# Two x tiles first on one queue: reordering the first loads and the first TensorE work of a gated attention/FFN kernel

## The chip, the cores and the metric

The kernel runs on one core of one Trainium2 chip. The metric is the device time of one execution in microseconds. A time is a median over runs, and two kernels are compared by runs on the same chip in the same rounds. The engines are TensorE (matrix products), VectorE and ScalarE (elementwise work), GpSimd and SyncE (here it only issues loads). A load (DMA) is put on the queue of the engine that issues it: in the traces of before one queue moved 0.82 MB, which is the five tiles of 160 KB that ScalarE issued. The profile counts 16 DMA engines, and its DMA share is the mean over them. A counter, a semaphore, tells of each load's progress; for a tile it is raised 16 times. A tile has landed with its sixteenth report.

## The reference, cut to what matters

```python
x = A_x                                   # (1, 2048, 640) bf16
g = sigmoid((x * gate_w).sum(-1))         # one gate per row
qkv = x @ wqkv                            # 640 -> q, k, v of 640 columns each
pq, pk = phi(q), phi(k)                   # phi(t) = t+1 if t>0 else exp(t), + 1e-6
a = linear_attention(pq, pk, v) @ wo      # 32 heads of 20
b = (gelu(x @ w_gate) * (x @ w_up)) @ w_down
out = g * a + (1 - g) * b
```

The change touches only the start. The rows of `x` come in 16 tiles of 128 rows. For each tile the kernel projects keys and queries with weights that come in five chunks of 128 rows each: `wk` 0 to 4 for keys, `wq` 0 to 4 for queries. One x tile and one weight chunk are each 160 KB.

## The kernel before: the parts that matter

Tiles 0 and 1 are loaded as they are and transposed on TensorE (`T`). Tiles 2 to 15 come through DMA transposes, and the first of these is issued when `wk` chunk 4 has landed. `KM` is a key projection of tile 0 or 1 over given chunks, `QM` the query projection, and `KQ` the joint projection of a tile from 2 on. `warm` issues matmuls whose results nobody reads; they fill waits.

```python
# loads: two issuing queues, SyncE ("sp", the default) and ScalarE ("act")
P.op("act", ... dma_start(touch[0:16, 0:4], A_wqkv[0:128:8, 640:644]))   # a 128-byte first load
load_x(0)
load_wk(0)
load_x(1, "act")
load_wk(1)
load_wk(3)
P.op("act", ... activation(eg[:, 0:1], zero, ACT.Exp))
load_wk(2, "act")
load_wk(4, "act")
P.op("dve", lambda e: e.memset(gw_sb, 0.0), writes=[r_gw])
dma_in(gw_sb[0:5, :], gate_w..., [r_gw], eng="act")
for k in range(KC):                        # KC = 5
    load_wq(k, ("sp", "act")[k % 2])
for i in range(NXN, NT):                   # tiles 2 to 15
    load_xT(i, after=([r_wk[4]] if i == NXN else ()))
...
# TensorE
warm(5, 512)
warm(1, 128)
T(0, [0], 7)                 # transpose of chunk 0 into PSUM bank 7, then a VectorE copy
T(0, [1, 2, 3, 4], 6)
warm(6, 128)
KM(0, [0])
T(1, [0], 7)
T(1, [1, 2, 3, 4], 6)
warm(3, 128)
KM(1, [0])
for k in (1, 2, 3):
    KM(0, [k])
    KM(1, [k])
gate_col()
for k in (4,):
    KM(0, [k])
    KM(1, [k])
for n in range(4):           # tiles 0 and 1: keys, then queries
    if n == 2:
        for k in range(KC):
            QM(2, [k])
            QM(3, [k])
    phi1(n)                  # ScalarE
    phi2(n)                  # VectorE
for i in range(2, NT):
    KQ(i)
...
```

Of the kernel before, what the change touches and what calls it, by code (L numbers as in the profile page):

```python
# [16 lines left out]
KC = D // 128  # L17
# [144 lines left out]
def bass_gated_mix__linear_attn_block__geglu_ffn__prompt_kernel(  # L162
# [63 lines left out]
    with (  # L226
# [8 lines left out]
        with contextlib.ExitStack() as stack:  # L235
            dma_sems = [stack.enter_context(nc.semaphore("s_in%d" % i)) for i in range(n_dma_in)]

            P = _Plan(["pe", "act", "dve", "pool", "sp"])
# [9 lines left out]
            def new_dma_key():  # L248
                k = "in%d" % dma_next[0]
                dma_next[0] += 1  # L250
                return k

            def v16(o, n):
                return pool[:, o:o + n]
# [13 lines left out]
            wk = wkq[:, :, 0:640]  # L268
            wq = wkq[:, :, 640:1281]
# [30 lines left out]
            gw_sb = v16(O_GW, 128)  # L300
# [4 lines left out]
            r_xn = [P.sb("xn%d" % i, R_XN + i * XW, R_XN + (i + 1) * XW) for i in range(NT)]  # L305
# [3 lines left out]
            r_wk = [P.sb("wk%d" % k, R_WK + k * WW, R_WK + k * WW + 640) for k in range(KC)]  # L309
            r_wq = [P.sb("wq%d" % k, R_WK + k * WW + 640, R_WK + k * WW + 1280) for k in range(KC)]  # L310
# [26 lines left out]
            r_gw = P.res("gw")  # L337

            def dma_in(dst, src, writes, reads=(), eng="sp"):
                P.op(eng, lambda e, dst=dst, src=src: e.dma_start(dst, src),  # L340
                     reads=reads, writes=writes, dma=new_dma_key())
# [3 lines left out]
            def load_x(i, eng="sp"):  # L345
                dma_in(x_aug[:, i, 0:640], A_x[0, i * 128:(i + 1) * 128, :], [r_xn[i]], eng=eng)

            def load_wk(k, eng="sp"):
                dma_in(wk[:, k, :], A_wqkv[k * 128:(k + 1) * 128, 640:1280], [r_wk[k]], eng=eng)

            def load_wq(k, eng="sp"):
                dma_in(wq[:, k, 0:640], A_wqkv[k * 128:(k + 1) * 128, 0:640], [r_wq[k]], eng=eng)


            P.op("act", lambda e: e.dma_start(touch[0:16, 0:4], A_wqkv[0:128:8, 640:644]),
                 writes=[P.res("touch")], dma=new_dma_key())
            load_x(0)
            load_wk(0)
            load_x(1, "act")
            load_wk(1)  # L360
            load_wk(3)

            zero = nc.const_aps.tensor(0.0, (128, 1), F32)
            P.op("act", lambda e: e.activation(eg[:, 0:1], zero, ACT.Exp), writes=[r_eg[0]])
            load_wk(2, "act")
            load_wk(4, "act")
            P.op("dve", lambda e: e.memset(gw_sb, 0.0), writes=[r_gw])
            dma_in(gw_sb[0:5, :], gate_w.rearrange("(k p) -> k p", p=128), [r_gw], eng="act")
            for k in range(KC):
                load_wq(k, ("sp", "act")[k % 2])  # L370

            def load_xT(i, after=()):
                P.op("sp", lambda e: e.dma_start_transpose(xT[:, :, i * 128:(i + 1) * 128],
# [12 lines left out]
            for c in range(NHC):  # L386
# [9 lines left out]
                 reads=[r_ones], writes=[r_ident])  # L396
# [16 lines left out]
            def warm(count, n):  # L413
                def fn(e):
                    last = None
                    for w in range(count):
                        last = e.matmul(ps[:, 4, 0:n], one_l, one_r[:, 0:n], start=True, stop=True)
                    return last
                P.op("pe", fn, writes=[bank[4]])
# [4 lines left out]
            def slot(n):  # L424
                return SLOTS[n % 4]

            def T(i, ks, tb):
                def fn(e):
                    last = None
                    for n, k in enumerate(ks):  # L430
                        last = e.transpose(psb[:, tb, n * 128:(n + 1) * 128],
                                           x_aug[:, i, k * 128:(k + 1) * 128], ident)
                    return last
                P.op("pe", fn, reads=[r_xn[i], r_ident], writes=[bank[tb]])
                P.op("dve", lambda e: e.tensor_copy(
                    xT[:, ks[0]:ks[-1] + 1, i * 128:(i + 1) * 128],
                    psb[:, tb, 0:len(ks) * 128].rearrange("p (k s) -> p k s", k=len(ks))),
                    reads=[bank[tb]], writes=[r_xTa[i] if ks[0] == 0 else r_xT[i]])
# [4 lines left out]
            def KM(n, ks):  # L443
                i = seq[n][1]
                b0, b1 = slot(n)

                def fn(e):
                    last = None
                    for k in ks:
                        lhs = xT[:, k, i * 128:(i + 1) * 128]  # L450
                        e.matmul(ps[:, b0, :], lhs, wk[:, k, 0:512], start=(k == 0), stop=(k == KC - 1))  # L451
                        last = e.matmul(ps[:, b1, 0:128], lhs, wk[:, k, 512:640],
                                        start=(k == 0), stop=(k == KC - 1))
                    return last
                P.op("pe", fn, reads=[r_xTa[i] if i < NXN and ks == [0] else r_xT[i]] + [r_wk[k] for k in ks],
                     writes=[bank[b0], bank[b1]])
# [37 lines left out]
            def gate_col():  # L494

                P.op("pe", lambda e: e.matmul(ps[:, 7, 0:5], gw_sb, ident[:, 0:5], start=True, stop=True),
                     reads=[r_gw, r_ident], writes=[bank[7]])
                P.op("dve", lambda e: e.tensor_copy(wq[:, :, 640:641], ps[:, 7, 0:5].unsqueeze(2)),
                     reads=[bank[7]], writes=[r_gcol])
# [4 lines left out]
            warm(1, 128)  # L504
            T(0, [0], 7)
            T(0, [1, 2, 3, 4], 6)
            warm(6, 128)
            KM(0, [0])
            T(1, [0], 7)
            T(1, [1, 2, 3, 4], 6)  # L510
            warm(3, 128)
            KM(1, [0])
            for k in (1, 2, 3):
                KM(0, [k])
                KM(1, [k])
            gate_col()
            for k in (4,):
                KM(0, [k])
                KM(1, [k])
            for n in range(4):  # L520
# [42 lines left out]
            for i in range(2, NT):  # L563
                KQ(i)
                if i == 4:
                    late_constants()
            P.op("dve", lambda e: e.tensor_scalar(gg, eg, 0.5, 0.5, ALU.mult, ALU.add),
                 reads=r_eg, writes=[r_g])
            P.op("dve", lambda e: e.tensor_scalar(omg, eg, -0.5, 0.5, ALU.mult, ALU.add),
                 reads=r_eg, writes=[r_omg])  # L570
# [7 lines left out]
                 reads=[r_omg], writes=[r_od], dma=new_dma_key())  # L578
# [44 lines left out]
            def ME(g):  # L623
# [6 lines left out]
                for c in cs:  # L630
# [8 lines left out]
                 reads=r_pk[0:2], writes=[r_tmp[0]])  # L639
            for i in range(2, NT):  # L640
                P.op("dve", lambda e, i=i: e.tensor_tensor(zacc, zacc, pk[i], ALU.add),  # L641
                     reads=[r_tmp[0], r_pk[i]], writes=[r_tmp[0]])
# [283 lines left out]
```

## Time and profile before

Three runs of the kernel before gave 274.1, 275.38 and 274.25 us. In the trace of one more run (273.55 us, span 272.2 us) the start looks like this:

| event | us from the span's start |
|---|---|
| full clock on TensorE | 3.77 |
| unbroken stream of key projections begins | 5.18 |
| query projections of tiles 0 and 1 begin | 7.67 |
| joint projections (tile 2) begin | 10.39 |

The page says how the whole span is shared. The first number after an engine is its busy time; the last line shown is the chain of waits by engine.

```profile
span 272.2 us, 3426 instructions
...
PE 267.9 (98%) x1343; PEld 128.1 (47%) x1369; DVE 141.8 (52%) x251; ACT 75.9 (28%) x132; POOL 30.0 (11%) x28
...
PE 95%; DVE 2%; DMA 1%; issue 1%; ACT 1%; SPq 0%; DVEq 0%; ACTq 0%
```

In these lines DVE is VectorE, ACT ScalarE, POOL GpSimd, PE TensorE, PEld its weight loads, and a q stands for an engine's issuing of loads. TensorE bounds the kernel. Only time in which TensorE does nothing useful can be won, and at the start that is the time before the key stream.

Lines of TensorE's timeline of before. The columns are start, duration, engine, source line, operation, output and inputs, shape and count; in brackets is idle time just before and what ended it. L431 are transposes, L417 warm-up matmuls, L451 and L452 key projections, L466 query projections, L536 joint projections.

```profile
3.02 0.74 PE L431 MATMUL ps<-pool 128*128 128x128 bf16 x5
...
4.38 0.38 PE L451 MATMUL ps<-pool 128*128 128x512 bf16 x1 [0.21 <-DMA pool<-in_A_wqkv_dram]
...
4.64 0.44 PE L431 MATMUL ps<-pool 128*128 128x128 bf16 x5
...
5.18 0.39 PE L451 MATMUL ps<-pool 128*128 128x512 bf16 x1
...
7.67 0.38 PE L466 MATMUL ps<-pool 128*128 128x512 bf16 x1
...
10.39 1.89 PE L536 MATMUL ps<-pool 128*128 128x512 bf16 x8
```

Five transposes take 0.74 us at 3.02 and 0.44 us at 4.64. That is the clock: half rate first (0.107 us from one to the next), full rate later (0.055); the trace's record of full clock begins at 3.77.

### The profile page before, as it was taken

The numbers are of one execution on the slowest core, as the hardware profiler recorded it, in microseconds if no ns is written. First come the engines' busy times: TensorE is split into PE (matmuls) and PEld (weight loads), VectorE is DVE, ScalarE is ACT, GpSimd is POOL, SyncE is SP. The second block draws the span as 40 slices with busy tenths as digits, with TensorE's granted clock in tenths as the row PEclk, the third lists the DMA queues.
The fourth block names the chain that finished last, engine by engine and source line by source line (L and its number), as shares of the span: only waits on it lengthen the run. The fifth ranks groups of instructions, "written<-read, shape, count | busy, mean of one in ns | idle before, by whom it ended". The sixth has DMA issues, their size and how long they took to land.

```text
span 272.2 us, 3426 instructions
## 1 busy us (share of the span) xinstructions
PE 267.9 (98%) x1343; PEld 128.1 (47%) x1369; DVE 141.8 (52%) x251; ACT 75.9 (28%) x132; POOL 30.0 (11%) x28
## 2 busy tenths in 40 slices
PE   8999999999999999999999999999999999999997
PEld 4555555544445444444444444444444444444444
DVE  2689898997333335999999999634110000000200
ACT  2555555210422453332222232224011122121021
POOL 5000000003140002242332421000000000000000
PEclk9999999999999999999999999999999999999999
DMA  6776999500300011612221221272031110110211
GB/s 219 176 114 124 349 402 384 119 2 19 61 16 2 23 50 51 200 28 48 27 48 30 43 50 25 60 229 96 5 79 37 41 39 19 39 41 19 58 58 41
DMA packets 42208, 23.61 MB, mean 87 GB/s; under 512 B 31567, under 2 KB 40783, under 8 KB 42063
## 3 DMA queue, kind: packets, MB, share of 16 engines
q1 hardware_dynamic: 41429, 22.56, 30.5%
q10 hardware_dynamic: 762, 0.82, 0.8%
q8 instruction: 11, 0.18, 0.3%
q14 instruction: 6, 0.05, 0.1%
HBM read 13.83 MB, written 2.63 MB: 60 GB/s over the span
## 4 chain that ended last, share of the span: by engine, by line
PE 95%; DVE 2%; DMA 1%; issue 1%; ACT 1%; SPq 0%; DVEq 0%; ACTq 0%
PE ps L697 41%; PE ps L861 23%; PE ps L536 12%; PE ps L593 6%; PE ps L840 4%; PE ps L808 2%; PE ps L675 2%; PE ps L596 2%; DMA pool<-in_A_wqkv_dram 1%; PE ps L451 1%; PE ps L821 1%; PE ps L466 1%; DVE pool L490 1%; PE ps L718 1%; DVE pool L555 1%
## 5 line engine op out<-in xcount | busy, mean ns | idle before, releaser
L697 PE MATMUL ps<-pool 128*128 128x512 bf16 x510 | 113.0, 379 | 0.5
L697 PEld LDWEIGHTS ps<-pool 128*128 128x128 bf16 x520 | 50.4, 98 | 60.1
L861 PE MATMUL ps<-pool 128*128 128x512 bf16 (+2 forms) x300 | 62.4, 367 | 0.3
L703 ACT ACTIVATE pool<-ps 128x512 f32<-128x512 f32 x52 | 31.0, 597 | 73.1 <-PE ps L697 73.1
L705 DVE TENSOR_TENSOR pool<-ps,pool 128x512 bf16<-128x512 f32 x52 | 34.6, 689 | 31.7 <-PE ps L697 30.4
L861 PEld LDWEIGHTS ps<-pool 128*128 128x128 bf16 x306 | 29.1, 98 | 33.5 <-issue 0.4
L536 PE MATMUL ps<-pool 128*128 128x512 bf16 (+1 forms) x206 | 37.9, 344 | 0.2
L844 DVE TENSOR_TENSOR pool<-ps,pool 128x512 bf16<-128x512 f32 x4 | 2.8, 692 | 61.5 <-PE ps L840 61.5
L751 POOL TENSOR_TENSOR pool<-pool 128x640 f32<-128x640 bf16 x16 | 22.5, 1406 | 72.8 <-DVE pool L753 65.9
L868 ACT ACTIVATE pool<-ps,pool 128x512 bf16<-128x512 f32 (+1 forms) x16 | 10.9, 680 | 68.6 <-PE ps L861 68.6
L536 PEld LDWEIGHTS ps<-pool 128*128 128x128 bf16 x210 | 20.5, 98 | 17.5
L555 DVE SCALAR_TENSOR_TENSOR pool<-ps,pool 128x128 bf16<-128x128 f32 (+2 forms) x42 | 25.3, 603 | 2.4
L546 ACT ACTIVATE pool<-ps 128x640 bf16<-128x640 f32 x28 | 19.7, 703 | 18.1 <-DVE pool L555 10.6
L593 PE MATMUL ps<-pool 128*128 128x512 bf16 x76 | 19.2, 380 | 0.1
L761 DVE TENSOR_TENSOR pool<-pool 128x640 bf16<-128x640 bf16 x16 | 13.2, 825 | 0.6
L759 DVE TENSOR_SCALAR pool<-pool 128x32 f32<-128x32 f32 x16 | 12.8, 803 | 0.6
L753 DVE TENSOR_REDUCE pool<-pool 128x32 f32<-128x640 f32 x16 | 12.9, 809 | 0.0
L641 DVE TENSOR_TENSOR pool<-pool 128x640 f32<-128x640 f32 x14 | 11.6, 826 | 0.5
L840 PE MATMUL ps<-pool 128*128 128x512 bf16 x51 | 11.5, 380 | 0.1
L643 POOL PARTITION_ALL_REDUCE pool<-pool x1 | 4.0, 3971 | 60.7 <-DVE pool L641 60.7
L593 PEld LDWEIGHTS ps<-pool 128*128 128x128 bf16 x78 | 6.9, 98 | 7.2
L552 DVE TENSOR_SCALAR pool<-pool 128x640 bf16<-128x640 bf16 x28 | 9.1, 327 | 1.8 <-ACT pool L546 0.4
(70 smaller groups left out, 105.0 us busy)
## 6 DMA issues: line engine op xcount, KB each, us to landing
out_dram<-pool SPq DMA_DIRECT2D x19, 128.0 KB, 1.7
pool<-in_B_w_gate_dram SPq DMA_DIRECT2D x1, 2080.0 KB, 14.2
pool<-in_B_w_up_dram SPq DMA_DIRECT2D x1, 2080.0 KB, 18.8
pool<-in_A_x_dram SPq DMA_DIRECT2D x1, 1280.0 KB, 8.7
pool<-in_B_w_down_dram SPq DMA_DIRECT2D x1, 1120.0 KB, 6.1
pool<-omg_row SPq DMA_DIRECT2D x1, 1024.0 KB, 4.8
pool<-in_A_wqkv_dram SPq DMA_DIRECT2D x6, 160.0 KB, 4.4
pool<-in_A_x_dram SPq DMA_DIRECT2D x1, 960.0 KB, 5.8
```

The costliest lines, as they stand in the source:

```text
L536: last = e.matmul(ps[:, b + p, 0:c1 - c0], xT[:, k, i * 128:(i + 1) * 128], wkq[:, k, c0:c1], start=(k == 0), stop=(k == KC - 1))
L546: P.op("act", lambda e: e.activation(e_buf[m], ps_flat[:, o:o + 640], ACT.Exp), reads=banks, writes=[r_e[m]])
L555: P.op("dve", lambda e, c0=c0, c1=c1: e.scalar_tensor_tensor(dst[:, c0:c1], ps_flat[:, o + c0:o + c1], 1.0 + EPS, e_buf[m][:, c0:c1], ALU. ...
L593: last = e.matmul(ps[:, b, :], pk[i][:, c * 128:(c + 1) * 128], x_aug[:, i, 0:512], start=(i == 0), stop=(i == NT - 1))
L697: last = e.matmul(ps[:, b, :], w[:, k, fc * 128:(fc + 1) * 128], xT[:, k, j * 512:(j + 1) * 512], start=(k == 0), stop=(k == KC - 1))
L703: P.op("act", lambda e: e.activation(ge[n], ps[:, gb, :], ACT.Gelu_apprx_tanh), reads=[bank[gb]], writes=[r_ge[n]])
L705: P.op("dve", lambda e: e.tensor_tensor(hT[fc][:, j * 512:(j + 1) * 512], ps[:, ub, :], ge[n], ALU.mult), reads=[bank[ub], r_ge[n]], write ...
L751: P.op("pool", lambda e: e.tensor_tensor(tmp[n], pq[i], z_b, ALU.mult), reads=[r_pq[i], r_zb], writes=[r_tmp[n]])
L753: P.op("dve", lambda e: e.tensor_reduce(den[n], tmp[n].rearrange("p (h d) -> p h d", h=32), AX.X, ALU.add), reads=[r_tmp[n]], writes=[r_de ...
L761: P.op("dve", lambda e: e.tensor_tensor(pq[i].rearrange("p (h d) -> p h d", h=32), pq[i].rearrange("p (h d) -> p h d", h=32), den[n].unsqu ...
L840: last = e.matmul(ps[:, b, :], wd[:, fc, 512:640], hT[fc][:, j * 512:(j + 1) * 512], start=False, stop=(fc == NFC - 2), skip_group_check=True)
L861: last = e.matmul(ps[:, pb, 0:c1 - c0], lhs, rhs, start=False, stop=(q == len(rows) - 1), skip_group_check=True)
```

## The change

The intent: both x tiles are needed for the key stream, so load them first and behind one another. Let the weight chunks follow in the order of need, hold back what is not urgent until something urgent has landed, transpose both tiles at once, and drop the filler in between.

```diff
+            P.op("dve", lambda e: e.memset(gw_sb, 0.0), writes=[r_gw])
+            dma_in(gw_sb[0:5, :], gate_w..., [r_gw], eng="act")
             load_x(0)
+            load_x(1)
             load_wk(0)
-            load_x(1, "act")
             load_wk(1)
-            load_wk(3)
+            load_wk(2)
             ... Exp on ScalarE ...
-            load_wk(2, "act")
+            load_wk(3, "act", after=[r_xn[0]])
             load_wk(4, "act")
-            (memset and gate weight load were here)
             for k in range(KC):
-                load_wq(k, ("sp", "act")[k % 2])
+                load_wq(k, ("sp", "act")[k % 2], after=([r_wk[1]] if k == 0 else ()))
 ... TensorE ...
             T(0, [1, 2, 3, 4], 6)
-            warm(6, 128)
-            KM(0, [0])
             T(1, [0], 7)
-            T(1, [1, 2, 3, 4], 6)
-            warm(3, 128)
-            KM(1, [0])
-            for k in (1, 2, 3):
-                KM(0, [k])
-                KM(1, [k])
-            gate_col()
-            for k in (4,):
+            T(1, [1, 2, 3, 4], 5)
+            warm(1, 128)
+            for k in range(KC):
+                if k == 4:
+                    gate_col()
                 KM(0, [k])
                 KM(1, [k])
```

`after=` makes the issuing engine wait until that tile has landed. A queue is issued in program order, so SyncE's `wq` 2 and 4 wait behind `wq` 0 as well.

More of the change, by code (lines that the diff above doesn't have):

```diff
@@ L346, in load_x, with load_wk, load_wq @@
                 dma_in(x_aug[:, i, 0:640], A_x[0, i * 128:(i + 1) * 128, :], [r_xn[i]], eng=eng)
-            def load_wk(k, eng="sp"):
-                dma_in(wk[:, k, :], A_wqkv[k * 128:(k + 1) * 128, 640:1280], [r_wk[k]], eng=eng)
-            def load_wq(k, eng="sp"):
-                dma_in(wq[:, k, 0:640], A_wqkv[k * 128:(k + 1) * 128, 0:640], [r_wq[k]], eng=eng)
+            def load_wk(k, eng="sp", after=()):
+                dma_in(wk[:, k, :], A_wqkv[k * 128:(k + 1) * 128, 640:1280], [r_wk[k]], reads=after, eng=eng)
+            def load_wq(k, eng="sp", after=()):
+                dma_in(wq[:, k, 0:640], A_wqkv[k * 128:(k + 1) * 128, 0:640], [r_wq[k]], reads=after, eng=eng)
             P.op("act", lambda e: e.dma_start(touch[0:16, 0:4], A_wqkv[0:128:8, 640:644]),
                  writes=[P.res("touch")], dma=new_dma_key())
+            P.op("dve", lambda e: e.memset(gw_sb, 0.0), writes=[r_gw])
+            dma_in(gw_sb[0:5, :], gate_w.rearrange("(k p) -> k p", p=128), [r_gw], eng="act")
             load_x(0)
+            load_x(1)
             load_wk(0)
-            load_x(1, "act")
             load_wk(1)
-            load_wk(3)
+            load_wk(2)
             zero = nc.const_aps.tensor(0.0, (128, 1), F32)
             P.op("act", lambda e: e.activation(eg[:, 0:1], zero, ACT.Exp), writes=[r_eg[0]])
-            load_wk(2, "act")
+            load_wk(3, "act", after=[r_xn[0]])
             load_wk(4, "act")
-            P.op("dve", lambda e: e.memset(gw_sb, 0.0), writes=[r_gw])
-            dma_in(gw_sb[0:5, :], gate_w.rearrange("(k p) -> k p", p=128), [r_gw], eng="act")
             for k in range(KC):
-                load_wq(k, ("sp", "act")[k % 2])
+                load_wq(k, ("sp", "act")[k % 2], after=([r_wk[1]] if k == 0 else ()))
             def load_xT(i, after=()):
```

## The prediction

> **What bounds the kernel now.** TensorE does: the page gives PE 98% busy (267.9 of 272.2 us), and the chain of waits is 95% PE. The change touches the first 10 us only. In the timeline PE reaches its unbroken stream of projection matmuls at 5.18 us; the tile-2 projections start at 10.39 us. Before 5.18 the useful PE work is ten transposes and one k-chunk of tile 0; the rest is warm-up matmuls and waiting. The chain opens with a DMA piece of 2.98 us (wk chunk 0, issued 1.26), then 0.17 us of warm-up. The waits view shows 0.4 us for x tile 0, 0.2 for wk0, 0.4 for VectorE's transpose copy, 0.2 for wk1.
>
> Landing times from the trace's semaphore records: x0 2.96, wk0 4.24, x1 4.41, wk1 5.41, wk2 5.59, wk3 6.24, wk4 6.49, wq0 7.39, wq1 7.84, wq2 8.25; the DMA transpose of x tile 2 is issued at 6.51, on wk4's landing, and lands at 10.18. From 4.41 to 8.96 nine 160 KB tiles land, 0.51 us each: the queues are full. [...] So the change buys no bandwidth, only order.
>
> **What the change does.** x1 no longer shares with wk0. Estimate from 0.51 us a tile after 2.96: x1 3.5, wk0 4.0 to 4.2, wk1 4.6, wk2 5.2, wk3 5.5, wk4 5.9. Tile 1's transposes then run at about 3.65 (bank 7 copied at 3.60), its first copy (0.23) follows tile 0's second (ends 4.21), so tile 1's first chunk starts at about 4.5, not 5.18. From there to 10.34 PE is dense but for 0.27 us of transposes moved ahead of it. So 0.7 us is the most the start can give.
>
> Two later loads trim it. wq0 is now issued only after wk1 lands (about 4.6, not 2.65); with the fastest issue-to-landing of 2.2 us, and wq1 and wq3 sharing, it lands at about 7.1, where PE wants it near 7.0. And the tile-2 transpose (3.67 us to landing, 0.16 us of slack before) starts near 6.0: KQ of tile 2 cannot start before about 9.7. Both leave about 0.5 us. All of it is on the critical path: the other 262 us keep their order and follow earlier.
>
> **Predicted time:** 273.8 us, 0.45 us (0.2%) less than 274.25; 8 in 10 between 273.1 and 274.8. Faster by over 2%: 0.5%; within 2%: 98.5%; slower by over 2%: 1%.
>
> **What would show it.** Timeline: tile 1's transposes right behind tile 0's near 3.6; the first two-tile dense stream from about 4.5; QM from about 7.1 with a short wait for a wq load; first tile-2 projection at 9.8 to 9.9. SyncE's first DMA transpose at about 6.0.
>
> **What would make it wrong.** The clock: full speed comes at 3.77 us in this trace (transposes 0.107 us apart before, 0.055 after). [...] Or wq0, or the tile-2 transpose behind the later wq loads, lands later than estimated and all gain turns into that wait. The before runs spread 1.3 us, more than the effect.

The marked cuts are two statements that no run of this case shows: a reason given for "no bandwidth, only order", and what sets the moment of full clock, with a cost worked out from it. The sum is: 0.7 us at most from the start, less about 0.2 for the two later loads, 0.45 us taken; 274.25 less 0.45 is 273.8.

## More of the kernel before

The windows view of before, from 3 to 8 us. The columns are the stretch, its length, busy time of each engine, the granted clock, the DMA share, and at the end GB/s.

```profile
3.00:4.00 1.00, 1.00 (x13) 0.98 (x11) 0.43 (x2) 0.20 (x1) 0.93 (x2) 1.00 0.96 314
4.00:5.00 1.00, 0.79 (x12) 0.54 (x10) 0.32 (x2) 0.00 (x0) 0.57 (x3) 1.00 1.00 360
5.00:6.00 1.00, 1.00 (x11) 0.51 (x9) 0.55 (x2) 0.00 (x0) 0.00 (x0) 1.00 0.98 326
6.00:7.00 1.00, 1.00 (x9) 0.57 (x8) 0.00 (x0) 0.00 (x0) 0.00 (x0) 1.00 0.97 341
7.00:8.00 1.00, 1.00 (x10) 0.60 (x9) 0.18 (x1) 0.41 (x1) 0.00 (x0) 1.00 0.97 350
```

Mind two columns for later: DMA share is near 1 all the time, and the last column, what was moved, is 338 GB/s on average over these 5 us.

## The result, and the profile after

After: 274.60 us median (274.49 to 274.84, 6 runs). Before, over all six of its runs by then: 274.18 us (273.64 to 275.38). The ratio is 1.0013, 95% interval 0.9993 to 1.0033. A ratio is the mean time of one kernel's fast runs over that of the other's of the same rounds, so it is not quite the ratio of the medians. The time is the same within noise, if anything longer; the gain is not there.

The page of after, the lines that answer to those of before:

```profile
span 273.5 us, 3436 instructions
...
PE 269.1 (98%) x1361; PEld 127.7 (47%) x1361; DVE 141.8 (52%) x251; ACT 76.0 (28%) x132; POOL 30.0 (11%) x28
...
PE 97%; DMA 1%; SPq 0%; ACT 0%; DVE 0%; issue 0%
```

Nothing in it says where 1.3 us of span went (PE's instruction counts, 1343 before and 1361 after, do not help: after issues eight matmuls fewer, so at least 26 records are missing from before's trace). The timeline of TensorE says it (L531 is before's L536):

```profile
3.09 1.13 PE L431 MATMUL ps<-pool 128*128 128x128 bf16 x10
4.06 0.22 PE L417 MATMUL ps<-const-bfloat16-1.0 128*128 128x128 bf16 x1
5.04 0.39 PE L451 MATMUL ps<-pool 128*128 128x512 bf16 x1 [0.77 <-DMA pool<-in_A_wqkv_dram]
...
7.93 0.22 PE L452 MATMUL ps<-pool 128*128 128x128 bf16 x1
9.06 0.38 PE L466 MATMUL ps<-pool 128*128 128x512 bf16 x1 [0.91 <-DVE pool L486]
...
11.78 0.59 PE L531 MATMUL ps<-pool 128*128 128x512 bf16 x2
```

The ten transposes run behind one another as intended. Then TensorE waits for `wk` chunk 0 until 5.04 us, finishes the key stream at 8.15 (7.93 and 0.22), and stands still until 9.06. The joint projections start at 11.78 instead of 10.39 us, 1.39 us later; the span is 1.3 us longer. What follows takes the same time: span less the start of the joint projections is 261.8 us before and 261.7 after, and between 261.7 and 261.9 in all 14 traces. The start of the joint projections is therefore a good meter for every version. As device time of a profiled run less that start is about 263.1 us, before's median of 274.18 us stands for a typical start near 11.1 (an estimate from these two numbers), not the 10.39 of its first trace. The same subtraction places every run without a trace: before's six at about 10.5 to 12.3, after's six at 11.4 to 11.7 (estimates, good to about 0.1 us). One trace is one draw from such a spread, which matters for every trace below.

The wait of 0.91 us at 9.06 is put down to VectorE's L486. L486 happened to end at 8.99 us, but it works on the keys and the query projections need nothing from it. What they do need is `wq` 0. The semaphore records in the trace give its landing as 8.92 us. The landings, in us, against those of before and those of the prediction:

| tile | before: issued | before: landed | predicted for after | after: issued | after: landed |
|---|---|---|---|---|---|
| x1 | 1.22 | 4.41 | 3.5 | 1.25 | 3.53 |
| wk0 | 1.25 | 4.24 | 4.0 to 4.2 | 1.70 | 5.00 |
| wk1 | 1.70 | 5.41 | 4.6 | 2.18 | 5.43 |
| wk2 | 1.77 | 5.59 | 5.2 | 2.65 | 6.28 |
| wk3 | 2.18 | 6.24 | 5.5 | 3.06 | 6.44 |
| wk4 | 2.19 | 6.49 | 5.9 | 3.44 | 7.11 |
| wq1 | 3.29 | 7.84 | | 3.93 | 7.54 |
| wq3 | 3.67 | 8.96 | | 4.41 | 8.29 |
| wq0 | 2.65 | 7.39 | 7.1 | 5.45 | 8.92 |

Only x1 came as predicted. `wq` 0 is the eighth tile to land before and the tenth after: `wq` 1 and 3, on the other queue and not held back, passed it. The windows view of after shows the second thing:

```profile
3.00:4.00 1.00, 0.99 (x11) 0.70 (x10) 0.42 (x2) 0.33 (x2) 0.93 (x2) 1.00 0.86 234
4.00:5.00 1.00, 0.28 (x5) 0.10 (x2) 0.69 (x3) 0.00 (x0) 0.58 (x3) 1.00 0.89 266
5.00:6.00 1.00, 0.95 (x7) 0.57 (x8) 0.00 (x0) 0.00 (x0) 0.00 (x0) 1.00 1.02 336
6.00:7.00 1.00, 0.98 (x8) 0.42 (x6) 0.00 (x0) 0.00 (x0) 0.00 (x0) 1.00 0.91 243
7.00:8.00 1.00, 1.00 (x10) 0.49 (x7) 0.18 (x1) 0.08 (x1) 0.00 (x0) 1.00 0.98 310
```

The DMA share is still about 0.9, but the mean is 278 GB/s against 338. Only the second from 5 to 6 us (336) comes up to before's mean; in its first half both queues have work (by the trace's packet records 85 GB/s on SyncE's and 294 on ScalarE's). ScalarE's queue moves nothing big before about 4.4 us (its first tile was issued at 3.06), and SyncE's is nearly empty from 5.5 to 7 (12 GB/s; its next load waited for `wk` 1 until 5.45).

### The profile page after: what moved, and what is told of

It is laid out like the page before. It is cut to its first block, busy times and chain, and to the rows that moved or that the text cites. A ratio compares the mean times of both kernels' runs of the same rounds, so it can differ in the third digit from the quotient of the medians.

```text
span 273.5 us, 3436 instructions
## 1 busy us (share of the span) xinstructions
PE 269.1 (98%) x1361; PEld 127.7 (47%) x1361; DVE 141.8 (52%) x251; ACT 76.0 (28%) x132; POOL 30.0 (11%) x28
## 4 chain that ended last, share of the span: by engine, by line
PE 97%; DMA 1%; SPq 0%; ACT 0%; DVE 0%; issue 0%
PE ps L692 41%; PE ps L856 23%; PE ps L531 14%; PE ps L588 6%; PE ps L835 4%; PE ps L803 2%; PE ps L670 2%; PE ps L591 1%; DMA pool<-in_A_wqkv_dram 1%; PE ps L466 1%; PE ps L451 1%; PE ps L816 1%; PE ps L713 1%; PE ps L731 0%; SPq L340 0%; ACT pool L476 0%
## 5 line engine op out<-in xcount | busy, mean ns | idle before, releaser
L531 PE MATMUL ps<-pool 128*128 128x512 bf16 (+1 forms) x210 | 38.1, 344 | 0.0
L531 PEld LDWEIGHTS ps<-pool 128*128 128x128 bf16 x210 | 20.5, 98 | 17.5
L636 DVE TENSOR_TENSOR pool<-pool 128x640 f32<-128x640 f32 x14 | 11.6, 826 | 0.5
L835 PE MATMUL ps<-pool 128*128 128x512 bf16 x52 | 11.6, 379 | 0.0
```

What stands on the lines that cost most here:

```text
L531: last = e.matmul(ps[:, b + p, 0:c1 - c0], xT[:, k, i * 128:(i + 1) * 128], wkq[:, k, c0:c1], start=(k == 0), stop=(k == KC - 1))
L835: last = e.matmul(ps[:, b, :], wd[:, fc, 512:640], hT[fc][:, j * 512:(j + 1) * 512], start=False, stop=(fc == NFC - 2), skip_group_check=True)
```

## The experiments

Theory L says that the loads decide: fewer bytes moved, and `wq` 0 last in line. Theory P says that the new order of TensorE's work costs the time. Each kernel was timed in five rounds against before. All gave correct results.

### Control: before against itself

No edit.

> A control: the kernel before, unedited, timed against itself. Ratio 1.000 within 0.002. The six runs of before known so far spread from 273.64 to 275.38 us, those of after only from 274.49 to 274.84. If before has two ways of starting (for instance a late transpose of x tile 2, which had 0.16 us of slack in the one trace, or a later full clock), this second profile may show the tile-2 projections starting later than 10.39 us and a span up to 1 us longer than 272.2. If the first trace is typical they start at 10.3 to 10.5 us and the span is 272 to 272.5.

Measured: ratio 1.0005 (0.9990 to 1.0020), 274.24 against 274.18 us. In this second trace of before, the key stream starts at 5.50, the queries at 8.22 and the joint projections at 10.95 us, span 272.8. Two things are later than in the first trace: the clock is still at half rate at 5.2 us (transposes 0.107 us apart), and several tiles land later (`wk` 2 at 6.52 against 5.59, `wk` 4 at 7.36 against 6.49). So the trace that the prediction rested on was a good draw, 0.56 us better at the meter than this one.

### After without the gate on wq0

```diff
-  load_wq(k, ("sp", "act")[k % 2], after=([r_wk[1]] if k == 0 else ()))
+  load_wq(k, ("sp", "act")[k % 2], after=())
```

> The kernel after, but wq chunk 0 is issued at once behind wk chunk 2 on SyncE's queue, without the wait for wk chunk 1 to land. Theory L (the loads: the gate on wq0 and a single queue that moves less than two): wq0 is issued near 3.1 us instead of 5.45 and lands by 7.5 instead of 8.92; the query projections start at about 8.0 to 8.3 instead of 9.06, the tile-2 projections at about 10.7 to 11.0 instead of 11.78; 0.7 to 1.0 us (0.3%) less than after. Theory P (the new order of TensorE's work costs the time, not the loads): the start of the query projections stays within 0.2 us of 9.06. A third possibility, that the early wq0 only takes bandwidth from wk3 and wk4, would show as a key stream that ends 0.5 us or more after 7.94.

Measured: 275.06 us, ratio 1.0040 (1.0023 to 1.0056). `wq` 0 was issued at 3.12 and landed at 7.72 us, a little past theory L's 7.5, and the wait before the query projections is gone. But the joint projections start at 11.74 us, as in after. The third possibility came true: `wk` 4 now lands at 8.42 instead of 7.11, and the key stream ends 1.0 us later. Over 3 to 8 us the rate is 281 GB/s, as with the gate. Removing the gate moved the wait from one tile to another. The query projections start at 9.03, which by the letter is also what theory P asked; the trace shows why, a key stream held up by `wk` 4. The gate is not the whole cause; the rate is left.

### TensorE's new order on the loads of before

```diff
 (before, with after's TensorE block: T(0), T(1), warm(1), then KM by chunk)
```

> The loads of before with TensorE's order of after (both tiles transposed first, nine warm-up matmuls fewer, then the k-chunks in turn). Theory L: the loads decide, so this is before within 0.2 us: x tile 1 lands at 4.4, wk1 at 5.4, the key stream ends at 7.7, the tile-2 projections start at 10.3 to 10.6 us. Theory P: the stream starts late or runs at the half clock for want of filler, and the tile-2 projections start at 11 us or later, 0.6 us or more behind before.

Measured: 274.62 us, but from 273.74 to 276.78; ratio 1.0029 (0.9996 to 1.0061), unclear. In its trace the loads land as before, the rate is 347 GB/s, and the joint projections start at 10.71. Three runs lie at 275.0 us or above, and the run of 276.78 us has a granted clock of 0.994, the only one under 1.0 in these rounds. The line from 3 to 8 us:

```profile
3.00:8.00 5.00, 3.86 (x35) 2.40 (x34) 1.48 (x5) 0.29 (x2) 1.50 (x4) 1.00 1.01 347
```

The load part of theory L holds for the landings and the rate; the times do not exclude theory P, as the median is no lower than after's. The traced run is the second fastest of the six. The spread is a new finding and is taken up below.

### The new loads under TensorE's order of before

```diff
 (after, with before's TensorE block, filler included)
```

> The loads of after with TensorE's order of before. Theory L: the query projections wait for wq0, landing at 8.7 to 9.1, and start near 9.1; the tile-2 projections start at 11.6 to 12.0 us; the time is that of after within 0.3 us. Theory P: as before, the tile-2 projections at 10.3 to 10.6 us.

Measured: 274.78 us (274.36 to 274.96), ratio 1.0023 (1.0010 to 1.0036). `wq` 0 lands at 8.80, the query projections start at 8.93, the joint ones at 11.65 us; the rate is 279 GB/s. The line from 3 to 8 us:

```profile
3.00:8.00 5.00, 4.59 (x41) 3.06 (x40) 1.46 (x5) 0.33 (x2) 1.50 (x4) 1.00 0.89 279
```

The loads alone bring after's times, so theory P is not needed for them. It is not excluded as a second cost: the new order alone has as high a ratio (1.0029), but over widely spread runs.

### How much one queue moves

Theory Q: one queue alone moves less than two together. Theory S: the queue does not matter.

```diff
 two_queues (after's TensorE order, no gates), in order of need:
+  sp:  x0 wk0 wk2 wk4 wq1 wq3
+  act: touch x1 wk1 wk3 gate_w wq0 wq2 wq4
 one_queue (the same order of need):
+  sp:  x0 x1 wk0 wk1 wk2 wk3 wk4 wq0 wq1 wq2 wq3 wq4
+  act: touch gate_w
   (one_queue's Exp also waits for touch, so that this load is waited for)
```

> TensorE's order of after, no gates, and the loads in the order in which they are needed, alternating between the two queues (SyncE: x0, wk0, wk2, wk4, wq1, wq3; ScalarE: x1, wk1, wk3, gate weights, wq0, wq2, wq4). Theory Q (a queue that runs alone moves less than two together, so what costs after its time is that ScalarE's queue is empty until about 4.4 us and SyncE's from about 5.5 to 7): 310 GB/s or more between 4.5 and 8.5 us, wk0 by 4.5, wk4 by 6.6, wq0 by 7.5, tile-2 projections at 10.2 to 10.8 us, time at or under before. Theory S (the queues do not matter; single lagging engines or the removed gates do): wk4 at 7.1 us or later as in after and in its version without the wq0 gate, tile-2 projections at 11.4 us or later.

> TensorE's order of after, no gates, all twelve tiles on SyncE's queue alone in the order of need. Theory Q: about 250 GB/s through the whole of 3 to 9 us, wk4 at about 7, wq0 at 8 or later, wq4 later than 10 us, tile-2 projections at 11.5 to 13 us, over 0.5 us more than before. Theory S: 310 GB/s or more, wk4 by 6.5 and wq0 by 7.2 us (perfect order, no gates), tile-2 projections by 10.6 us.

The window from 3 to 8 us, two queues:

```profile
3.00:8.00 5.00, 4.35 (x30) 2.59 (x29) 1.29 (x4) 0.68 (x2) 1.50 (x4) 1.00 1.03 355
```

and one queue:

```profile
3.00:8.00 5.00, 4.76 (x33) 2.69 (x32) 1.30 (x5) 0.33 (x2) 1.50 (x4) 1.00 0.93 280
```

Theory Q holds for the rate: 355 against 280 GB/s with the same twelve tiles to load. The view counts all that was moved, the first DMA transposes too (issued at 5.82 with two queues, at 7.33 with one); in the seconds before those, from 3 to 5 us, it is 341 and 378 against 242 and 324. Why a lone queue is slower no run shows. It is not issue time: the one queue issued a tile every 0.47 us, which is 349 GB/s (163,840 bytes over 0.47 us), and the time from issue to landing grew from 2.25 us for x0 to 4.10 us for the last tile. Over all traces, 3 to 8 us:

| loads | GB/s in each trace |
|---|---|
| both queues from the start (seven traces) | 338, 330, 347, 347, 355, 342, 327 |
| after's queues with the gate on x0 (five traces) | 278, 265, 279, 281, 275 |
| one queue | 280 |
| after without any gate | 305 |

The consequence drawn for the times was too strong. The one queue landed `wq` 0 at 7.72 instead of 8 or later, because nothing passed it, and its joint projections started at 10.98, not 11.5 or later; 274.57 us, ratio 1.0018 (1.0005 to 1.0031). This trace is of the fastest of its five runs; by the subtraction above the others started at about 11.1 to 11.6. In it TensorE does not wait between key and query projections, although the rate is as low as after's. With two queues everything landed as expected (`wk` 0 4.21, `wk` 4 5.80, `wq` 0 7.73, a little later than the 7.5 expected), but the joint projections started at 11.26, and the runs lay from 273.79 to 276.15 us, ratio 1.0025 (0.9998 to 1.0052). That is a miss of theory Q, which asked for 10.8 at most and a time at or under before. Early loads did not make it fast. In its trace the first key projections of 512 columns hold TensorE for 0.43 us each instead of 0.22 until about 6.5 us: the half clock.

### Without the first small load

```diff
-  act: touch x1 wk1 ...
+  act: x1 wk1 ...
```

> The same without the small first load on ScalarE's queue, so x tile 1 is issued at 0.8 instead of 1.23 us. Theory Q: x1 lands at 3.0 to 3.3 us, everything behind it on that queue up to 0.45 us earlier, tile-2 projections at 9.8 to 10.4 us, 0.3 us less than with the small load. If the small load warms something that the weight loads need, wk0 lands later than 4.6 us instead and the gain is gone.

Measured: 274.63 us, ratio 1.0018 (1.0003 to 1.0033), no gain. Its joint projections started at 10.70 in the trace (of the fastest of its six runs) instead of 10.4 or earlier. x0 landed at 3.65 instead of 3.02 and x1 at 3.83, and `wk` 0 at 4.63, just past the bound given. That fits the small load having a use, but one trace does not show whether it warms anything, and x0, which was sent no earlier and no later, also came late. A rival was not tested: x0 and x1 are now sent at the same moment and may share the DMA engines. It stays open.

### After without both gates

```diff
-  load_wk(3, "act", after=[r_xn[0]])
+  load_wk(3, "act")
-  ... after=([r_wk[1]] if k == 0 else ()))
+  ... after=())
```

> After without both gates: wk3 and wk4 no longer wait for x0 to land, wq0 no longer for wk1. ScalarE's queue then starts at about 3.1 us instead of 4.4. Theory Q: wk4 lands at 6.4 to 7.0 instead of 7.11 (8.42 with the wq0 gate alone removed), wq0 by 8.0, tile-2 projections at 10.6 to 11.2 us. Theory S: no better than with only the wq0 gate removed, 11.7 us or later.

Measured: 275.13 us (274.20 to 276.64), ratio 1.0045 (1.0019 to 1.0071). In the trace the joint projections start at 13.65. By the letter that fits theory S (11.7 or later), but not for its reason. The profile fell on the slowest run, and its windows view shows what happened in it; the third number from the right is the granted clock:

```profile
6.00:7.00 1.00, 0.45 (x4) 0.11 (x2) 0.00 (x0) 0.00 (x0) 0.00 (x0) 0.96 0.88 293
7.00:8.00 1.00, 0.82 (x3) 0.39 (x4) 0.00 (x0) 0.00 (x0) 0.00 (x0) 0.50 1.01 369
8.00:9.00 1.00, 1.00 (x5) 0.52 (x4) 0.00 (x0) 0.00 (x0) 0.00 (x0) 0.50 0.47 154
9.00:10.00 1.00, 1.00 (x5) 0.52 (x4) 0.00 (x0) 0.00 (x0) 0.00 (x0) 0.50 0.87 141
10.00:11.00 1.00, 1.00 (x9) 0.51 (x7) 0.18 (x1) 0.15 (x1) 0.00 (x0) 0.83 0.61 117
```

The trace's clock records give full clock from 3.51 to 6.92 us, half from 6.92 to 10.34, full after that: two stretches of 3.413 us each. TensorE had stood idle from 4.26 to 5.73 and again from 6.44 to 7.18 us, so that it was busy for 1.42 of the 3.41 us before the clock fell. By what rule the clock fell and rose this trace does not show. Theory Q's part was half right: `wk` 4 landed at 7.35, a little past its bound. But `wk` 0 landed at 5.68, later than in after, with its eighth report at 4.35: with more bytes moved (305 GB/s from 3 to 8 us), a tile can still be late by its last reports.

### Is it the filler? (theory H)

```diff
 before_pe_order_filled, between the two tiles' transposes:
+  warm(10, 128)
 two_queues_filled, in the same place:
+  warm(8, 128)
```

> The loads of before and TensorE's order of after, with ten 128-column warm-up matmuls between the transposes of the two tiles, where TensorE sat idle for 1.4 us in the version without them (three of its six runs were at 275.0 us or more, one with a granted clock of 0.994). Theory H [...]: no run over 275 us, median 273.6 to 274.3, ratio to before 0.998 to 1.002. If the spread came from the loads alone, two or three of six runs are again at 275 us or more.

> The two-queue loads in the order of need, TensorE's order of after, and eight 128-column warm-up matmuls in its wait for x tile 1 (two of six runs without them were near 276 us, and its profile ran the first key projections 0.43 us apart instead of 0.22). Theory H: no run over 275 us; the key stream at full speed from its start near 4.8 to 5.0 us; tile-2 projections at 10.2 to 10.5; median 273.4 to 273.9, ratio to before 0.997 to 1.000, the best of all versions. If the loads alone decide, it is as without filler: 273.8 to 276.2 us.

Theory H says that where TensorE sits idle in the first 5 us, the key projections sometimes run at half speed.

| loads of | filler | runs, us | ratio to before (95%) |
|---|---|---|---|
| before | no | 273.74 to 276.78, 3 of 6 at 275.0 or more | 1.0029 (0.9996 to 1.0061) |
| before | yes | 273.52 to 274.37, none | 0.9984 (0.9969 to 0.9999) |
| two queues | no | 273.79 to 276.15, 2 of 6 | 1.0025 (0.9998 to 1.0052) |
| two queues | yes | 273.77 to 275.19, 1 of 6 | 0.9998 (0.9981 to 1.0016) |

On the loads of before all came as theory H asked, and the six runs fell together. For the two queues the filler narrowed the spread but one run still passed 275 us, against the expectation; the joint projections of its trace started at 11.03, not by 10.5, and the version is as fast as before, not the best of all. Together that is one run of twelve at 275.0 us or more with filler against five of twelve without, on different chips. It speaks for theory H but does not show it. Filler does not make the clock come at a fixed time: in the trace of before_pe_order_filled the half clock lasts until about 6.2 us although TensorE was busy throughout, from 0.82 on, while in the trace of the version without filler full clock is on record from 3.67 and an idle stretch of 1.14 us before 4.90 did not end it. Filler may make a late full clock rarer; these two traces do not show it.

### After again, and after with wq0 on the other queue

```diff
-  load_wq(k, ("sp", "act")[k % 2], after=([r_wk[1]] if k == 0 else ()))
+  load_wq(k, ("act", "sp")[k % 2], after=([r_wk[1]] if k == 1 else ()))
```

> A control: the kernel after, unedited, beside the next three on one chip. Ratio to before 1.001 to 1.003. If its first profile is typical: wk0 lands at 4.6 to 5.2 us, wq0 (tenth tile to land) at 8.7 to 9.2, the query projections start at 8.9 to 9.2 with TensorE idle 0.6 us or more before them, the tile-2 projections at 11.6 to 12.0.

> After with the wq chunks swapped between the queues: wq0, wq2 and wq4 on ScalarE's queue behind wk4, wq1 and wq3 on SyncE's with the gate on wk1. Theory O (in after wq0 is overtaken by wq1 and wq3 and lands tenth; that is the query wait): wq0 lands eighth, at 7.3 to 7.8 us, the query projections start at 7.9 to 8.3; then wq1, now the late one (8.5 to 8.9), takes back about 0.4 us, so the tile-2 projections start at 11.0 to 11.4, 0.3 to 0.7 us less than after. If instead the bytes alone decide (every order of the same tiles ends equally late), the tile-2 projections start at 11.6 us or later and the time is that of after.

After again: 274.86 us against 274.44, ratio 1.0015 (1.0002 to 1.0028). So after is slower by about 0.15%, 0.4 us. `wk` 0 landed at 4.78, `wq` 0 at 9.25, a little later than expected, tenth again; the query projections started at 9.39 and the joint ones at 12.11, also a little late. This time the waits view names the load itself (columns: who waited, for what, total us, times, longest):

```profile
PE ps L466 <- DMA pool<-in_A_wqkv_dram: 1.3, 1, 1.3
```

With the swap, `wq` 0 landed eighth, at 7.50 us, as theory O said, and the query projections no longer wait for it. But theory O's forecast of the time failed: the median is 274.91 us, ratio 1.0023 (1.0009 to 1.0036), and the profiled run (275.61 us, the slowest of its six) has the joint projections at 12.53. TensorE's timeline of that run:

```profile
4.26 0.31 PE L417 MATMUL ps<-const-bfloat16-1.0 128*128 128x128 bf16 x1
5.13 0.61 PE L451 MATMUL ps<-pool 128*128 128x512 bf16 x1 [0.56 <-DMA pool<-in_A_wqkv_dram]
...
8.84 0.51 PE L451 MATMUL ps<-pool 128*128 128x512 bf16 x1
...
9.27 0.38 PE L451 MATMUL ps<-pool 128*128 128x512 bf16 x1
...
9.81 0.38 PE L466 MATMUL ps<-pool 128*128 128x512 bf16 x1
```

A key projection of 512 columns shows 0.61 us at 5.13 and 0.38 at 9.27: the half clock lasted until 9.09, which is where the trace's clock record begins. TensorE had waited from 4.57 to 5.13 us for `wk` 0; whether that wait made the full clock late is not shown. The granted clock in the windows view reads 1.00 from 5 to 9 us, where the key projections of 512 columns take 0.61 to 0.63 us but for the last (0.51); that column shows the half clock of the start in none of the 14 traces (their clock records begin with the full clock, or there are none), and one has to read it from the spacing of the matmuls. So one wait was taken away and the profiled run met another delay, the half clock. The other five runs (274.78 to 275.10 us) have no trace; by the subtraction above they started at about 11.7 to 12.0, not at theory O's 11.0 to 11.4. Whether the clock held them as well is open.

## Why the prediction was right or wrong

The measured 274.60 us lies in the range, 0.8 us above the 273.8 predicted. That is luck of a range 1.7 us wide, which took in no change at all; the path to the number was wrong. "Within 2%" was right; the expected small gain was not there, and two timings of after against before lie on the other side of 1 (1.0013 and 1.0015).

- **What bounds the kernel, and that the rest only follows: right.** 261.7 to 261.9 us follow the start of the joint projections in all 14 traces.
- **"So the change buys no bandwidth, only order": this step failed.** It took 0.51 us a tile from a stretch in which both queues had work and used it where one queue was empty. After moves 278 GB/s from 3 to 8 us against 338 before. The experiment with one queue against two shows that an empty queue lowers the rate: 280 against 355 GB/s with the same tiles. With it `wk` 0 to 4 land at 5.00 to 7.11, not 4.0 to 5.9, the key stream starts at 5.04, not 4.5, and most of the 0.7 us at the start is not won. The rate is not the only cause of a late `wk` 0, as the next point and the version without both gates (305 GB/s, `wk` 0 at 5.68) show.
- **Landing was treated as a single moment per tile: also too simple.** A tile is complete with the last of its 16 reports. `wk` 0 had its eighth report at 4.02 us and its last at 5.00 in after; before it was 3.96 and 4.24. So the forecast 4.0 to 4.2 held for half of the reports. In the traces of before and after the last report of a tile came from 0.05 to 0.97 us after the eighth, and for `wk` 0 in after without both gates 1.33 us. It varies from run to run and is part of why single traces of one kernel differ.
- **"It lands at about 7.1" for `wq` 0: the term that was mis-sized most.** It landed at 8.92. `wk` 1, its gate, landed 0.83 us later than assumed (5.43 against 4.6), and from issue it took 3.47 us where the sum left about 2.5, with `wq` 1 and 3 landing ahead of it. That gave a wait of 0.91 us between key and query projections, where a "short wait" was forecast. The swap showed that order can mend the landing (7.50). Removing the gate showed that it cannot be mended for nothing (`wk` 4 paid). Neither shortened the time (274.91 and 275.06 us).
- **The transpose of tile 2 as a second limit: not seen.** It landed at 11.06 in after, 0.72 us before its use.
- **The clock as the way it could go wrong: right in kind, not shown as the cause in after.** In after's first trace TensorE was at full rate by 3.8 us (transposes 0.107 us apart to 3.49, 0.055 from 3.78). The half clock cost several of the variants dearly: traces show it in the slowest run of after without gates, in the `wq` 0 swap until 9.09 and in the two-queue loads until about 6.5 us, and one run of the new TensorE order without filler has a granted clock of 0.994. The other runs at 275 us and more have no trace, but for one of after (275.10), whose full clock is on record only from 5.11. What sets the moment the runs do not settle: in the traces told here full clock came from 3.5 to about 6.5 us, and in the swap at 9.09. That after's own runs lie so close (274.49 to 275.10 over twelve runs) may be because its wait for `wq` 0 hides a late clock; that is argued, not shown.
- **The size of the baseline.** The forecast started from a trace in which the joint projections begin at 10.39, and from a median of 274.25 us that stands for about 11.1. That is why a delay of 1.39 us between two traces is only about 0.4 us between the timings.

Where the expected gain went: x1 did come 0.9 us earlier. In after's traces it is lost in the waits for `wk` 0 and `wq` 0, which go with the lower load rate and the gate; after's loads alone, under the old TensorE order, are slower than before as well (1.0010 to 1.0036). But no version without filler that mended one of these won the time back, and in the traces of several of them part of the key stream ran at the half clock; so how the loss divides between rate, order and clock stays open. The TensorE half of the change may be sound if filler is kept: on before's loads it is 0.16% faster than before (0.0001 short of no difference at the interval's edge), 273.98 against 274.44 us, and after took 274.86 in the same rounds. It is the only one of the eleven versions whose interval lies below 1, and only just, so it should be timed again before it is believed.

## What to carry to other kernels

When loads limit a start, keep both issuing queues supplied from the first moment and express priority by the order within the queues. Here that raised the rate (355 GB/s from 3 to 8 us against 280 from one queue), but without filler it did not shorten the time (ratio 1.0025). A gate that holds a load back until another has landed can empty a queue, as it did here (SyncE's moved 12 GB/s from 5.5 to 7 us), and puts the held load behind whatever was not held (`wq` 0 landed tenth, at 8.92 us). Keep TensorE busy through load waits of the first microseconds: with filler one run of twelve was at 275.0 us or more, without it five of twelve, though no run shows why. And before trusting a slack of 0.2 us, look at a second trace of the same kernel.
